# A planned transformer kernel: the opening's costs in the plan, the port shared by VectorE and GpSimd, and all orders chosen anew

## The chip, the cores and the metric

The kernel runs on one core of a Trainium2 chip. Each core has engines that work side by side, each through its own queue in order: TensorE (PE, with its weight loads PEld), VectorE (DVE), ScalarE (ACT), GpSimd (POOL) and SyncE (SP), which here issues the DMAs. The metric is the device time of one execution in microseconds (us); lower is better.

## The reference, cut to what matters

Two attention blocks over 2048 positions, 1024 channels and 32 heads of 32, whose outputs are concatenated.

```python
# A: four segments of 512; a causal softmax in the segment, and a memory of those before
q, k, v = x @ wq, x @ wk, x @ wv
for s in range(4):
    a_dot = softmax(qs @ ks.T * scale + mask) @ vs
    a_mem = (phi(qs) @ M) / (phi(qs) @ z + 1e-6)      # phi(t) = t + 1 if t > 0 else exp(t)
    o = g * a_mem + (1 - g) * a_dot                   # g = sigmoid(beta), one per head
    M, z = M + phi(ks).T @ vs, z + phi(ks).sum()
out_a = o @ wo
# B: linear attention with a learned feature map
q, k, v = split(x @ wqkv)
f = lambda t: concat(softmax(t @ w_phi), softmax(-t @ w_phi))   # per head
kv, z = f(k).T @ v, f(k).sum()
out_b = (f(q) @ kv) / (f(q) @ z + 1e-6) @ wo
```

## The kernel before, in words

Every large product is made of float16 halves: an operand is scaled by its largest magnitude, rounded to float16 (`hi`, on ACT), and what is left is rounded too (`lo`, on DVE or POOL); `product` then adds hi*hi, hi*lo and lo*hi in PSUM, so 128x128 by 128x512 is three matmuls. The B block's large products use a seven-product (Strassen) scheme, `strassen`, and A's output projection at the end another.

Stages in time: the opening (loads, scales and halves of the first segment and weights); the A block, 32 units of a segment and a group of four heads (`produce`, `attend`, with `fold`, which multiplies w_phi into B's weights, between them), up to about 850 us; B's pass over keys and values, up to about 1185; B's pass over queries, up to about 1515; A's output projection (L1719).

The order of the work is planned. Each operation is not issued where it is written but recorded by `op(engine, planned duration, function, r=reads, w=writes, prio=...)`. When all are recorded, `Graph.run` plays a greedy list schedule while the program is built: every engine is free from 0; again and again the operation that can start earliest is taken, among several the one of the smallest priority; its function then emits the instruction (or nothing, if it does nothing). So the plan fixes the order of each engine's queue and the PSUM banks, and on the chip the queues run in that order, each instruction waiting for its inputs. What the plan knows:

- durations, and latencies between engines (`LAT`: DVE to ACT 0.16 us, DVE to PE 0.4);
- for a DMA (engine SP): 0.6 us to issue, then its kilobytes over `FLOW` = 230 per us, one after the other, then `lat`;
- `port=True`: such a DVE operation and any POOL operation exclude each other, one starts after the other has ended;
- `NUDGE`: operations are counted off in stretches of 60; for a stretch with a number in `NUDGE` each priority is shifted by a pseudo-random amount drawn from that number, of a reach of 0.3 to 3.0;
- where PE would idle for over `GAP` = 0.5 us, `fill` inserts spare matmuls (L380) by a rule on how much PE has worked lately.

Instructions of the preparation (masks, the identity, the selector `sel`, cleared buffers: L337 to L377) are emitted before the graph and are unknown to its plan.

What the texts speak of in the opening: `load_seg(0)` loads the first segment of x in eight pieces (L469, `S<-ax`), reduces each to its largest magnitude (DVE L485) and then all (L495, `xam`); `scale` sums and spreads that with a matmul (PE L433) and makes the scale and its inverse (DVE L435, L437); `halves` makes hi (ACT L449) and lo (DVE L451). `load_wg(0)` does the same for the first group's key weights with ACT L491 (absolute sum), L433, L435, then POOL L443, ACT L445, POOL L446. `fold(-1)` loads `quad` (L1175) and scales it (L1192). The `stk` buffers get four constant rows each from `sel` (ACT L659, twelve copies). The first projection is `produce(0)`, L422. `phib` holds w_phi and is loaded by L1113 into a cleared buffer (L340); `mem` is A's memory (cleared at L1111).

Around 1190 us the sums of the keys, `za`, are turned into factors (`zr` L1508, L1510, L1511; `zs` L1513), the keys' product is scaled (L1516) and halved (ACT L1519, DVE L1521), and the queries' products (L618) and exponentials (DVE L1320 to L1330, ACT L1327, POOL L1624) begin; `keep` copies a product from PSUM (ACT L624). L1568 makes a scale of the output projection.

Of the kernel before, what the change touches and what calls it, by code (L numbers as in the profile page):

```python
# [12 lines left out]
AF = mybir.ActivationFunctionType  # L13
OP = mybir.AluOpType
AX = mybir.AxisListType
# [30 lines left out]
NUDGE = {0: 820989, 2: 102852, 3: 529656, 4: 266905, 5: 924189, 6: 435410, 9: 911235, 12: 450738, 13: 124130, 14: 669972,  # L46
# [59 lines left out]
class Graph:  # L106
# [36 lines left out]
    def op(self, eng, dur, fn, r=(), w=(), prio=0, lat=0.0, short=False, port=False, need=(), kb=256):  # L143
        o = Op()
# [163 lines left out]
def tile_kernel(ctx: ExitStack, tc: tile.TileContext, ax, aw, awv, awo, beta, bx, bwqk, bwv, bphi, bwo, out):  # L308
    nc = tc.nc
# [69 lines left out]
    G = Graph(pools)  # L379
# [14 lines left out]
    for i in range(NG):  # L394
        op(POOL, 0.358, lambda i=i: nc.gpsimd.tensor_tensor(
            bdm[:, i, :, 0:32], hd[:, :, None].to_broadcast([128, 4, 32]),
            gate[:, 4 * i:4 * i + 4, None].to_broadcast([128, 4, 32]), op=OP.mult), r=[gates], w=[(bdmb, i)], prio=0.3)
        op(DVE, 0.071, lambda i=i: nc.vector.tensor_reduce(bdm[:, i, :, 32], hd[:, :, None], axis=AX.X, op=OP.add), w=[(bdmb, i)], prio=0.3)
# [256 lines left out]

    stk = [G.buf("slot", [128, 2, 4, 512], F16, f"S{12 + i}") for i in range(3)]
    for t in stk:
        for h in range(4):
            op(ACT, 0.5, lambda t=t, h=h: nc.scalar.activation(t()[96:104, 1, h], sel[96:104, h:h + 1].to_broadcast([8, 512]), AF.Copy),  # L659
               w=[(t, (1, 3, h))], prio=0.3)  # L660
# [450 lines left out]
    op(POOL, 1.19, lambda: nc.gpsimd.memset(mem, 0.0), w=[phib, memb], prio=-1)  # L1111
# [24 lines left out]
    def fold(n, prio, dep=()):  # L1136
# [35 lines left out]
        if n < 0:  # L1172
# [18 lines left out]
            for k in range(4):  # L1191
                op(ACT, 0.5, lambda k=k: nc.scalar.activation(qd()[:, k], qd()[:, k], AF.Copy, scale=si()[:, 1:2]),  # L1192
                   r=[si], w=[(qd, k)], prio=0.5)
# [312 lines left out]
    for hb in range(2):  # L1506
        zr, zs, v = G.buf("b", [128, 8], F32, "zr", 2), G.buf("b", [128, 8, 2], F32, "zs", 2), slice(8 * hb, 8 * hb + 8)
        op(DVE, 0.172, lambda zr=zr, v=v: nc.vector.tensor_scalar(zr(), za()[:, v], 1e-12, None, op0=OP.max),  # L1508
           r=[(za, (hb, 0)), (za, (hb, 1))], w=[zr], prio=P)
        op(DVE, 0.12, lambda zr=zr: nc.vector.reciprocal(zr(), zr()), w=[zr], prio=P)  # L1510
        op(DVE, 0.141, lambda zr=zr: nc.vector.tensor_scalar(zr(), zr(), osc2[:, 1, 1:2], 2.0, op0=OP.mult, op1=OP.mult),  # L1511
           r=[(oscs, 1)], w=[zr], prio=P)
# [46 lines left out]
    def sizes_out(j, prio):  # L1559
        t = blocks(j, prio)  # L1560
        for k in range(2):
            for h in range(2):
                op(ACT, 0.614, lambda k=k, h=h: nc.scalar.activation(
                    t[k]()[:, h], t[k]()[:, h], AF.Abs, accum_out=ast()[:, 4 * j + 2 * k + h:4 * j + 2 * k + h + 1]),
                   w=[(t[k], h), (ast, (j, k, h))], prio=prio)
        if j == 3:
            scale((ast, ast), 16, (wscs, (2, 0), lambda: wsc[:, 2, 0]), prio, "s", 13)
            op(DVE, 0.1, lambda: nc.vector.tensor_tensor(wsc[:, 2, 1, 0:1], wsc[:, 2, 0, 0:1], osc2[:, 0, 0:1], op=OP.mult),  # L1568
               r=[(wscs, (2, 0)), (oscs, 0)], w=[(wscs, (2, 1))], prio=prio)
# [243 lines left out]
```

## Time and profile before

| | us |
|---|---|
| median of 3 runs (lowest, highest) | 1667.47 (1667.42, 1668.37) |
| the profiled execution | 1668.69 |
| its span | 1667.0 |
| PE busy | 1648.0 |
| DVE, ACT, POOL busy | 1357.1, 1111.7, 1059.3 |

The span reaches from the first instruction to the end of the last; the rest of the execution's time lies around it. In rows of instructions: start, length, engine, line, operation, out<-in, shape, count, and in brackets the engine's idle time before it with what ended it. Rows of one kind in sequence are merged into one (x8). A matmul's length holds its way through the array, so the distance between starts tells the rate.

### The profile page before, as it was taken

The numbers are of one execution on the slowest core, as the hardware profiler recorded it, in microseconds if no ns is written. First come the engines' busy times: TensorE is split into PE (matmuls) and PEld (weight loads), VectorE is DVE, ScalarE is ACT, GpSimd is POOL, SyncE is SP. The second block draws the span as 40 slices with busy tenths as digits, with TensorE's granted clock in tenths as the row PEclk, the third lists the DMA queues.
The fourth block names the chain that finished last, engine by engine and source line by source line (L and its number), as shares of the span: only waits on it lengthen the run. The fifth ranks groups of instructions, "written<-read, shape, count | busy, mean of one in ns | idle before, by whom it ended". The sixth has DMA issues, their size and how long they took to land.

```text
span 1667.0 us, 35571 instructions
## 1 busy us (share of the span) xinstructions
PE 1648.0 (99%) x12922; PEld 967.2 (58%) x12922; DVE 1357.1 (81%) x3213; ACT 1111.7 (67%) x2044; POOL 1059.3 (64%) x1393
## 2 busy tenths in 40 slices
PE   8999999999999999999999999999999999999999
PEld 7666767667676666766754444445544444444444
DVE  6899989899896888897877898988997787975441
ACT  8798779868787777777865767645755464454431
POOL 3967577576777886967874454545799897640000
PEclk9999999999999999999999999999999999999999
DMA  6845556779456462756566354276466665753311
GB/s 232 239 139 157 154 158 171 202 201 247 111 161 164 131 176 90 197 190 179 155 203 260 121 197 170 86 255 246 173 151 150 166 181 158 214 149 136 121 57 64
DMA packets 265599, 279.68 MB, mean 168 GB/s; under 512 B 162768, under 2 KB 216016, under 8 KB 256848
## 3 DMA queue, kind: packets, MB, share of 16 engines
q1 hardware_dynamic: 265424, 277.42, 56.0%
q8 instruction: 101, 1.65, 0.4%
q14 instruction: 74, 0.61, 0.1%
HBM read 143.34 MB, written 85.00 MB: 137 GB/s over the span
## 4 chain that ended last, share of the span: by engine, by line
PE 73%; DVE 10%; POOL 8%; ACT 4%; DMA 2%; issue 2%; SPq 0%; DVEq 0%; ACTq 0%; POOLq 0%
PE proj L422 25%; PE proj L618 11%; PE misc L422 6%; PE proj L1719 5%; PE s L1034 4%; PE pv L1070 4%; PE s L941 3%; PE s L618 3%; PE s L1719 2%; POOL e L1624 2%; PE misc L618 2%; POOL e L1636 1%; DVE mx L1320 1%; PE misc L1215 1%; PE misc L1719 1%
## 5 line engine op out<-in xcount | busy, mean ns | idle before, releaser
L422 PE MATMUL proj<-S,S 128*128 128x512 f16 (+1 forms) x2304 | 494.1, 343 | 0.6 <-ACT S L449 0.2
L422 PEld LDWEIGHTS <-S 128*128 128x128 f16 x3072 | 288.1, 98 | 160.3 <-ACT S L449 0.7
L618 PE MATMUL proj<-S,S 128*128 128x512 f16 x1488 | 344.2, 380 | 5.8 <-ACT cs L624 4.7
L618 PEld LDWEIGHTS <-S 128*128 128x128 f16 x1968 | 187.5, 98 | 220.1 <-issue 9.1
L1047 POOL TENSOR_SCALAR_AFFINE_SELECT ph<-ph 128x256 f16<-128x256 f16 (+1 forms) x448 | 194.7, 458 | 109.2 <-DVE ph L1041 94.9
L1041 DVE SCALAR_TENSOR_TENSOR ph<-s,ph 128x512 f16<-128x512 f32 x320 | 208.5, 683 | 51.7 <-ACT ph L1040 46.0
L947 DVE CUSTOM_DVE_ANT_0 s<-s,causal 128x384 f32<-128x384 f32 (+3 forms) x512 | 241.1, 509 | 8.5 <-PE s L941 5.9
L1040 ACT ACTIVATE ph<-s 128x512 f16<-128x512 f32 x320 | 185.3, 647 | 0.7
L422 PE MATMUL misc<-S,ot 128*128 128x512 f16 x768 | 171.0, 379 | 0.0
L1327 ACT ACTIVATE e<-e,sk 128x256 f32<-128x256 f32 x256 | 114.2, 497 | 61.1 <-DVE e L1324 39.9
L422 PEld LDWEIGHTS <-ot 128*128 128x128 f16 x768 | 73.8, 98 | 88.3
L1038 ACT ACTIVATE s<-s,bdl 128x512 f32<-128x512 f32 x160 | 105.7, 702 | 21.4 <-PE s L1034 21.1
L1038 ACT ACTIVATE s<-s,bd 128x512 f32<-128x512 f32 x160 | 103.0, 689 | 20.9 <-PE s L1034 14.9
L1034 PE MATMUL s<-S 104*128 104x512 f16 (+3 forms) x512 | 113.2, 299 | 0.0
L941 PE MATMUL s<-S 96*128 96x512 f16 (+3 forms) x512 | 112.0, 299 | 0.7 <-DVE dm L994 0.3
L422 PE MATMUL proj<-wv,S 128*128 128x256 f16 x768 | 101.2, 272 | 0.0
L1070 PEld LDWEIGHTS <-ph 128*128 128x128 f16 x2560 | 88.8, 96 | 18.8 <-POOL ph L1047 0.8
L1624 POOL TENSOR_TENSOR e<-e,zb 128x512 f32<-128x512 f32 x64 | 84.1, 1329 | 16.2 <-DVE r L1330 13.2
L1070 PE MATMUL pv<-vl,ph 128*128 128x66 f16 (+1 forms) x2560 | 92.2, 184 | 0.0
L1330 DVE TENSOR_REDUCE r<-e 128x32 f32<-128x1024 f32 x64 | 76.5, 1204 | 12.3 <-ACT e L1327 12.0
L618 PE MATMUL s<-S,S 128*128 128x512 f16 x324 | 78.6, 379 | 0.4 <-DVE S L451 0.4
L947 DVE DVE_READ_ACCUMULATOR2_ANT mt<- 128x1 f32 x512 | 71.7, 140 | 0.0
(375 smaller groups left out, 3303.2 us busy)
## 6 DMA issues: line engine op xcount, KB each, us to landing
S<-h SPq DMA_DIRECT2D x192, 128.0 KB
S<-wf_d SPq DMA_DIRECT2D x21, 1024.0 KB
st<-bwqk SPq DMA_DIRECT2D x56, 256.0 KB
wf_d<-fo SPq DMA_DIRECT2D x48, 256.0 KB
out<-os SPq DMA_DIRECT2D x38, 256.0 KB
wf_d<-oT SPq DMA_DIRECT2D x36, 256.0 KB
S<-xf_d SPq DMA_DIRECT2D x9, 1024.0 KB
S<-aw SPq DMA_DIRECT2D x16, 512.0 KB
```

The lines of the kernel that those rows point to most:

```text
L422: op(PE, dur, lambda c=c, a=a, b=b, lv=lv, rv=rv: nc.tensor.matmul(pv(), lv(), rv(), start=(c == 0 and a + b == 0), stop=(c == n - 1 and a ...
L618: op(PE, 0.2165, lambda n=n, a=a, b=b, lv=lv, rv=rv: nc.tensor.matmul(ps(), lv(), rv(), start=(start and n == 0 and a + b == 0), stop=(n = ...
L941: nc.tensor.matmul(ps()[:, o:o + 128 * i + 128], st()[0:96, 0, h, 128 * i:128 * i + 128], st()[0:96, 1, h, 0:128 * i + 128], start=True, s ...
L947: dve({128: 0.216, 256: 0.381, 384: 0.6, 512: 0.648}[n], lambda h=h, i=i, o=o, n=n: nc.vector.tensor_tensor_reduce(ps()[:, o:o + n], ps()[ ...
L1034: nc.tensor.matmul(ps()[:, o:o + n], st()[0:104, 1, h, 128 * j:128 * j + 128], st()[0:104, 0, h, 128 * j:512], start=True, stop=True)
L1038: act(0.571, lambda: nc.scalar.activation(ps(), ps(), AF.Exp, bias=0.0, scale=bd()[:, 4, i2, 0:1]), r=[(bd, i2)], w=[ps])
L1040: act(0.478, lambda: nc.scalar.activation(ph()[:, 0], ps(), AF.Copy, scale=2.0 ** 14), r=[ps], w=[(ph, 0)])
L1041: dve(0.6, lambda: nc.vector.scalar_tensor_tensor(ph()[:, 1], ps(), 2.0 ** 14, ph()[:, 0], op0=OP.mult, op1=OP.subtract), r=[ps, (ph, 0)], ...
L1047: nc.gpsimd.affine_select(pd, pd, pattern=[[0, n], [1, 128]], compare_op=OP.is_ge, fill=0.0, base=0, channel_multiplier=-1)
L1070: nc.tensor.matmul(ps()[:, i, n0:n1], ph()[:, a, o:o + 128], vl()[:, j, h4 + h, n0:n1], start=(i == 0 and a == 0), stop=(j == min(i, 2)), ...
L1624: op(POOL, 1.23, lambda a=a, h0=h0, e=e: nc.gpsimd.tensor_tensor(e()[:, 8 * a:8 * a + 8], e()[:, 8 * a:8 * a + 8], zv()[:, h0:h0 + 8], op= ...
L1719: op(PE, 0.2165, lambda n=n, a=a, b=b: nc.tensor.matmul(ps(), v(a)[:, n, :], wform[w]()[:, b, n, :], start=(start and n == 0 and a + b == ...
```

## The change

No instruction is added or taken away; the durations and dependences of the plan change, and with them the order of the queues (the number of filling matmuls may differ too).

- DMAs of a priority of -2 or below (the opening's): 0.47 us to issue, 0.65 of their kilobytes, 0.5 us more to land.
- Five stand-ins with no instruction, first in the plan: DVE 3.5 us, which "writes" `sel` and which the L659 copies now wait for; POOL 1.4 us, which "writes" `phib`, and 0.9; PE 0.8; ACT 0.5. The clearing of `mem` no longer stands as a writer of `phib`.
- L398 is planned at 0.1 instead of 0.071, L1192 at 0.62 instead of 0.5.
- L1508, L1511 and L1568 have `port=True`.
- All of `NUDGE` is another set of numbers (149 stretches before, 154 after).

```diff
-NUDGE = {0: 820989, 2: 102852, 3: 529656, 4: 266905, 5: 924189, 6: 435410, 9: 911235, 12: 450738, 13: 124130, 14: 669972,
...
+NUDGE = {0: 410426, 4: 742560, 5: 453547, 8: 418033, 11: 31061, 12: 825983, 13: 702578, 14: 361939, 15: 102890, 16: 584341,
...
     def op(self, eng, dur, fn, r=(), w=(), prio=0, lat=0.0, short=False, port=False, need=(), kb=256):
+        if eng == "SP" and prio <= -2:
+            dur, kb, lat = 0.47, 0.65 * kb, lat + 0.5
...
-        op(DVE, 0.071, lambda i=i: nc.vector.tensor_reduce(bdm[:, i, :, 32], hd[:, :, None], axis=AX.X, op=OP.add), w=[(bdmb, i)], prio=0.3)
+        op(DVE, 0.1, lambda i=i: nc.vector.tensor_reduce(
+            bdm[:, i, :, 32], hd[:, :, None], axis=AX.X, op=OP.add), w=[(bdmb, i)], prio=0.3)
...
+    selb = G.fixed(sel)
+    op(DVE, 3.5, lambda: None, w=[selb], prio=-99)
     stk = [G.buf("slot", [128, 2, 4, 512], F16, f"S{12 + i}") for i in range(3)]
     for t in stk:
         for h in range(4):
             op(ACT, 0.5, lambda t=t, h=h: nc.scalar.activation(t()[96:104, 1, h], sel[96:104, h:h + 1].to_broadcast([8, 512]), AF.Copy),
-               w=[(t, (1, 3, h))], prio=0.3)
+               r=[selb], w=[(t, (1, 3, h))], prio=0.3)
...
-    op(POOL, 1.19, lambda: nc.gpsimd.memset(mem, 0.0), w=[phib, memb], prio=-1)
+    op(POOL, 1.4, lambda: None, w=[phib], prio=-99)
+    op(POOL, 0.9, lambda: None, prio=-98)
+    op(POOL, 1.19, lambda: nc.gpsimd.memset(mem, 0.0), w=[memb], prio=-1)
+    op(PE, 0.8, lambda: None, prio=-99)
+    op(ACT, 0.5, lambda: None, prio=-99)
...
-                op(ACT, 0.5, lambda k=k: nc.scalar.activation(qd()[:, k], qd()[:, k], AF.Copy, scale=si()[:, 1:2]),
+                op(ACT, 0.62, lambda k=k: nc.scalar.activation(qd()[:, k], qd()[:, k], AF.Copy, scale=si()[:, 1:2]),
...
         op(DVE, 0.172, lambda zr=zr, v=v: nc.vector.tensor_scalar(zr(), za()[:, v], 1e-12, None, op0=OP.max),
-           r=[(za, (hb, 0)), (za, (hb, 1))], w=[zr], prio=P)
+           r=[(za, (hb, 0)), (za, (hb, 1))], w=[zr], prio=P, port=True)
...
         op(DVE, 0.141, lambda zr=zr: nc.vector.tensor_scalar(zr(), zr(), osc2[:, 1, 1:2], 2.0, op0=OP.mult, op1=OP.mult),
-           r=[(oscs, 1)], w=[zr], prio=P)
+           r=[(oscs, 1)], w=[zr], prio=P, port=True)
...
             op(DVE, 0.1, lambda: nc.vector.tensor_tensor(wsc[:, 2, 1, 0:1], wsc[:, 2, 0, 0:1], osc2[:, 0, 0:1], op=OP.mult),
-               r=[(wscs, (2, 0)), (oscs, 0)], w=[(wscs, (2, 1))], prio=prio)
+               r=[(wscs, (2, 0)), (oscs, 0)], w=[(wscs, (2, 1))], prio=prio, port=True)
```

31 rows, old and new, of the table NUDGE are left out of this document.

## The prediction

> **What bounds the kernel now.** I read the head and the chain of the profile first, then the busy time by stretches, then the two stretches in which TensorE is idle, engine by engine.
>
> ```profile
> span 1667.0 us, 35571 instructions
> PE 1648.0 (99%) x12922; PEld 967.2 (58%) x12922; DVE 1357.1 (81%) x3213; ACT 1111.7 (67%) x2044; POOL 1059.3 (64%) x1393
> PE 73%; DVE 10%; POOL 8%; ACT 4%; DMA 2%; issue 2%; SPq 0%; DVEq 0%; ACTq 0%; POOLq 0%
> ```
>
> TensorE (PE) is the bound: busy for 1648.0 of 1667.0 us. The change emits no instruction and removes none, so it can only move TensorE's idle time, its clock, and its warming and filling products. Where the idle time lies (columns: stretch, length, busy time of PE, of the weight loads, of DVE, ACT, POOL, the granted clock, DMA):
>
> ```profile
> 0.00:17.06 17.06, 13.11 (x78) 12.85 (x79) 9.01 (x24) 11.49 (x21) 8.72 (x17) 0.90 0.91 320
> 17.06:60.00 42.94, 42.07 (x285) 28.37 (x282) 33.77 (x126) 34.73 (x66) 25.18 (x36) 1.00 0.62 197
> 60.00:1180.00 1120.00, 1114.34 (x9641) 698.44 (x9640) 978.91 (x2564) 839.64 (x1565) 773.83 (x1064) 1.00 0.59 176
> 1180.00:1225.00 45.00, 40.70 (x305) 22.93 (x304) 43.79 (x78) 26.65 (x60) 32.11 (x37) 0.96 0.49 141
> 1225.00:1550.00 325.00, 324.86 (x2102) 153.64 (x2100) 249.85 (x366) 163.59 (x282) 219.47 (x242) 1.00 0.59 162
> ```
>
> The first projection starts at 17.06 us; what PE does before is warming, filling and a few small sums, so nearly all of these 17.06 us is lost. After that PE idles 0.87 us up to 60, 5.66 us in the 1120 us up to 1180, 4.30 us in the 45 us around 1200 (where the keys' pass hands over to the queries' pass), and 0.14 us up to 1550. The prize is thus two places and a thin rest of some 6 us.
>
> **The opening.** First what TensorE waits for, then ACT, DVE and the loads:
>
> ```profile
> 10.06 0.38 PE L433 MATMUL misc<-wgb,one 128*128 128x1 f32 x2 [1.79 <-ACT S L491]
> 15.58 0.28 PE L433 MATMUL misc<-xam,one 128*128 128x1 f32 x2
> 17.06 0.38 PE L422 MATMUL proj<-S,S 128*128 128x512 f16 x1
> ...
> 4.59 4.24 ACT L659 ACTIVATE S<-sel 8x512 f16<-8x512 f32 x8 [2.53 <-DVE sel L372]
> 8.86 1.06 ACT L491 ACTIVATE S<-S 128x1024 f16<-128x1024 f32 x1
> ...
> 4.95 0.69 DVE L485 TENSOR_REDUCE twb<-S 128x1 f32<-128x512 f32 x1 [0.40 <-DMA S<-ax]
> 6.64 0.69 DVE L485 TENSOR_REDUCE twb<-S 128x1 f32<-128x512 f32 x1 [1.00 <-DMA S<-ax]
> 10.47 0.16 DVE L435 TENSOR_SCALAR wgs<-misc 128x1 f32<-128x1 f32 x1 [3.15 <-PE misc L433]
> 10.75 3.63 DVE L485 TENSOR_REDUCE twb<-S 128x1 f32<-128x512 f32 x6
> 14.41 0.16 DVE L495 TENSOR_REDUCE xam<-twb 128x1 f32<-128x8 f32 x1
> ...
> 0.79 0.39 SPq L469 DMA_DIRECT2D S<-aw  x1
> 1.24 0.89 SPq L469 DMA_DIRECT2D S<-ax  x2
> 2.17 0.92 SPq L1113 DMA_DIRECT2D phib<-bphi  x2
> 3.14 3.82 SPq L469 DMA_DIRECT2D S<-ax  x6
> 11.00 0.33 SPq L1175 DMA_DIRECT2D quad<-bwqk  x1
> ...
> 1.70 4.92 DMA S<-ax
> 6.63 0.33 SPq L469
> ...
> 11.01 3.13 POOL L443 TENSOR_SCALAR S<-S,wgs 128x512 f32<-128x512 f32 x2 [6.96 <-DVE wgs L437]
> ```
>
> Read from the end. The projection at 17.06 needs x halved, which needs the largest |x| (L495, 14.41), which needs eight reductions (L485), one for each load of x. Two of them ran as their loads landed; then DVE stood 3.15 us at L435, the scale of the first weights, with six reductions queued behind it, which then ran back to back. L435 waited for the product at 10.06, that for ACT's absolute sum L491 at 8.86, and L491 stood behind eight copies of L659, which could not start before DVE had made `sel` (4.59, after 2.53 us of waiting). So eight copies that nobody needs yet, put ahead by a plan that believes DVE free at zero, hold up the scale chain for 4.24 us.
>
> What does the data allow? The chain of work has the third load land at 6.62 and the eleventh issue at 6.63: an issue waits for the landing eight issues before it. The issue at 11.00 is the nineteenth, so it waited for the eleventh, the last piece of x: that landed at about 10.98. A reduction takes 0.69, so the last one could end near 11.7 instead of 14.38 (10.75 + 3.63): 2.7 us. The weights were issued at 0.79, ahead of all x; if they landed no later than the third load, L491 could start by 6.62 instead of 8.86, L435 would follow near 8.2 (10.47 less 2.24), and the six reductions behind it would end at 12.1: still 2.2 us gained. If they landed with the first load of x, which released the reduction at 4.95, the landing at 10.98 alone sets the end.
>
> What the edits do there, each by itself:
> - The 3.5 us stand-in on DVE, which writes `sel`, with the copies reading it: in the plan the copies are ready at 3.66, not 0. L491 and the copies now come in an order that knows of it. This is the edit that can win the 2.7 us. The twelve copies keep their time; ACT has idle time for them until the halves begin at 16.29.
> - Loads of the opening at 0.47 us an issue instead of 0.6: the trace has two issues in 0.89 and two in 0.92. Bytes at 0.65: 256 KB become 0.72 us in the plan instead of 1.11; between the landings at 6.62 and 10.98 lie six loads of x and two small ones, 4.36 us or 0.73 a load of x. The plan's x now lands about when the chip's does, so reductions are queued where the data are. Worth nothing alone; the 2.7 us need it, since with the old rates the plan would expect x later than it comes.
> - The stand-ins on POOL (1.4 and 0.9), PE (0.8) and ACT (0.5) and the freeing of the `phib` loads from the clearing of `mem`: they shift planned starts only; POOL sat idle for 6.96 us before 11.01, which covers any of these shifts. Nothing, and without that cover at most the 1.19 us at which the plan priced the clearing.
> - 0.62 for the four scalings L1192 and 0.1 for the eight reductions L398: below, nothing.
>
> ```profile
> 37.44 2.55 ACT L1192 ACTIVATE quad<-quad,sif 128x512 f32<-128x512 f32 x4
> L398 DVE TENSOR_REDUCE bdm<-hd x8: 142/151/155, 37.4 to 52.9; 128x4 f32<-128x4 f32 x8
> ```
>
> They take 0.64 and 0.15 each; eight times 0.03 and four times 0.12 correct the plan by 0.7 us on engines that are not the bound there.
>
> Does a start 2.7 us earlier last? From 17.06 to 60 PE idles only 0.87 us, and its feeders in that stretch start from the same x scale, so they move with it. I take 2.7. Ends: 0 (a later load or POOL's weight chain holds PE at the old time) and 3.4 (also the 0.7 us that the product at 15.58 came after L495's end at 14.57 plus a semaphore).
>
> **The handover around 1190.** PE, the clock by stretches, then DVE beside POOL, then ACT:
>
> ```profile
> 1198.39 5.84 PE L618 MATMUL proj<-S,S 128*128 128x512 f16 x19 [2.26 <-ACT cs L624]
> ...
> 1194.79:1198.20 3.41, 1.33 (x7) 0.49 (x5) 2.87 (x7) 3.41 (x9) 0.00 (x0) 1.00 0.01 2
> 1198.20:1201.62 3.42, 3.23 (x8) 1.13 (x8) 3.42 (x6) 3.39 (x11) 3.29 (x4) 0.50 0.10 20
> 1217.40:1220.80 3.40, 2.05 (x14) 1.25 (x13) 3.40 (x9) 2.18 (x5) 0.72 (x2) 1.00 0.68 154
> ...
> 1188.46 1.09 DVE L1511 TENSOR_SCALAR zr<-zr,osc 128x8 f32<-128x8 f32 x1
> 1192.69 0.98 DVE L1508 TENSOR_SCALAR zr<-za 128x8 f32<-128x8 f32 x1
> 1188.25 2.50 POOL L1624 TENSOR_TENSOR e<-e,zb 128x512 f32<-128x512 f32 x2 [2.66 <-ACT zb L1500]
> 1192.05 1.59 POOL L1624 TENSOR_TENSOR e<-e,zb 128x512 f32<-128x512 f32 x1 [1.30 <-DVE r L1330]
> ...
> 1196.84 0.62 ACT L1519 ACTIVATE st<-ez 128x512 f16<-128x512 f32 x1
> 1197.76 0.58 ACT L624 ACTIVATE cs<-proj 128x512 f32<-128x512 f32 x1
> ```
>
> The plan prices L1511 at 0.141 and L1508 at 0.172. Beside POOL they took 1.09 and 0.98; the L1508 ended at 1193.67, just after POOL's product (1193.64). So DVE is 1.76 us later than planned, ACT's copies L1519 in their fixed order later too, and behind them stands L624, the copy that empties PE's bank: PE idles 2.26 us. Then the clock is granted at half: eight products in 3.42 us, where 48 elsewhere take 10.36:
>
> ```profile
> 994.08 10.36 PE proj L618 x48
> ```
>
> That is 1.7 us for the eight. The stall's bill is 2.26 + 1.7 = 4.0 us. With these operations marked as sharing POOL's port, the plan puts them after POOL's product, puts others ahead, and orders ACT by the true times. A stall of 1.35 us in the stretch from 1217.40 left the clock at 1.00, so I take the least change that spares the clock: 2.26 falls to 1.35 (0.9) and the half-rate stretch goes (1.7): 2.6. Ends: 0 and 4.0. The wait exists in the plan alone; but behind an operation that the plan places too late stand the reductions and subtractions of the queries' exponentials, and ACT's L1327 and L624 wait for those: DVE was busy for 43.79 of 45 us, so a misplaced one costs its 0.6 to 1.2 us again. L1568, marked too, frees nobody on PE's path: nothing.
>
> [...]
>
> **All orders chosen anew.** Every stretch gets another random shift, so the rest is drawn afresh. It can win at most the idle time that is there, 5.66 + 0.14 us, and can lose as much or more. Nothing in the trace tells the sign: I take 0, ends -2.9 (half of it) and +5.8 (the same again).
>
> **The sum.** The profiled execution took 1668.69: a span of 1667.0 and 1.69 around it. Less 2.7 and 2.6 it is 1663.4. The median of the runs, 1667.47, lies 1.2 below the profiled one: 1662.2.
>
> **Rivals.**
> - A. Both places win more: 3.4, 4.0, and the 1.35 us of the second stall, 8.8 less: 1658.7; with some of the thin rest, 1657. For it: the stall's cause is the mispriced step. Against: DVE is full there. 0.13.
> - B. The gain stays in the opening or gets lost: the x scale comes earlier, but PE then waits for the second weights, which POOL prepares (POOL busy 25.18 of 42.94), and the handover stalls in another way. 1665 (all but 0.2 of the opening's 2.7, nothing else) to 1667.5 (nothing). For it: lists are greedy, and one missing input stops a queue as before. Against: 0.87 us of idle time up to 60 shows no tight feeder. 0.26.
> - C. Slower: a new order lets PE stand over 2 us, with the half rate behind it, 4.0 us each by the handover's bill. One is less than the 5.3 forecast; from three on (12) the kernel is slower by over 0.2%: 1667.5 - 5.3 + 12.0 = 1674. In 1120 us the trace shows idle time of 5.66 in all and no half rate, which speaks against. 0.13.
>
> **Numbers.** A measurement tells about 0.2%, 3.3 us, from no change. Forecast 0.48 (own range 1659.5 to 1664), A 0.13, B 0.26, C 0.13. Faster: the forecast and A, 0.61; same: B; slower: C. The range from 1657 to 1668 leaves out C and a little of A and B, under 0.2 together.
>
> **What would show it.** Right: L491 ahead of most of the L659 copies and starting by 6.6; L495 near 12; the first projection near 14.4; no half rate near 1200. A half-rate stretch reaching past the first projection would cost up to 1.7 us. Wrong: the projection starts at 17 as before, or the first of PE's idle time moves to 17 to 60; PE idle in 60 to 1180 above 9 us would make C.

## The result, and the profile after

The changed kernel takes 1680.01 us (median; 1678.95 to 1680.97), the kernel before, on the same chip, 1667.92 (1667.42 to 1668.95): a ratio of 1.0072, 95% interval 1.0060 to 1.0085. It is slower by 12.1 us; the prediction said 1662.2. The profiled execution took 1680.19 with a span of 1678.5.

Head and chain of the profile after:

```profile
span 1678.5 us, 35518 instructions
...
PE 1648.9 (98%) x12902; PEld 961.8 (57%) x12902; DVE 1362.2 (81%) x3213; ACT 1114.3 (66%) x2044; POOL 1067.0 (64%) x1393
...
PE 35%; DVE 14%; POOL 6%; ACT 4%; issue 2%; DMA 2%; SPq 0%; ACTq 0%; DVEq 0%; POOLq 0%
```

TensorE is busy as long as before (1648.9 against 1648.0): no work was added, it only stands still more. By stretches, with the same columns and, but for the first projection's start, the same cuts as before:

```profile
0.00:16.08 16.08, 11.62 (x72) 11.24 (x73) 10.44 (x25) 12.93 (x23) 8.76 (x17) 0.92 0.90 318
16.08:60.00 43.92, 43.71 (x277) 27.93 (x278) 34.53 (x124) 34.55 (x67) 25.11 (x36) 0.95 0.66 203
60.00:1180.00 1120.00, 1104.67 (x9555) 689.90 (x9554) 966.73 (x2548) 834.80 (x1548) 763.37 (x1052) 1.00 0.57 174
1180.00:1225.00 45.00, 43.34 (x304) 24.28 (x302) 42.28 (x79) 29.48 (x68) 35.22 (x41) 1.00 0.51 170
1225.00:1550.00 325.00, 321.42 (x2125) 152.42 (x2124) 261.66 (x375) 162.76 (x283) 234.54 (x248) 1.00 0.58 163
```

Both places that the change aims at did improve: the projection starts at 16.08 instead of 17.06, and the handover has 1.66 us of idle time instead of 4.30, at full clock. But between 60 and 1180 TensorE idles 15.33 us instead of 5.66. Now set the instants of the two traces beside each other at equal work of TensorE done (the columns of its products, warming and filling ones left out; good to about half a microsecond). The changed kernel is 2.1 us ahead at 60, 2.5 behind at 300, 3.8 at 600, 9.0 at 900, 11.4 at 1180, 7.8 at 1200, 11.0 at the end. The loss comes in the long middle, bit by bit, which the change touched only through its new orders: the operations whose costs it corrected run before 60 or after 1180 us. Behind the handover it loses once more (3.58 us of idle time from 1225 to 1550 instead of 0.14); no experiment takes that stretch by itself.

The waits of TensorE from 60 to 1180 (line, what it waited for: us in total, times, longest); before, the two largest, and after, the six largest:

```profile
PE proj L618 <- ACT cs L624: 1.1, 1, 1.1
PE proj L618 <- ACT pq L624: 0.9, 2, 0.6
```

```profile
PE misc L975 <- DVE mh L970: 1.8, 1, 1.8
PE s L947 <- DVE mt L953: 1.5, 2, 0.8
PE proj L622 <- ACT pq L628: 1.5, 2, 1.0
PE s L1040 <- DVE ph L1047: 1.2, 2, 0.8
PE proj L622 <- ACT cs L628: 1.2, 2, 1.0
PE s L622 <- DVE S L455: 1.0, 1, 1.0
```

No single stall: many sorts of work, once or twice each, mostly ended by VectorE. Adding up the gaps over 0.1 us by what ended them gives VectorE 3.4 us before and 10.3 after, ScalarE 2.0 and 3.3, GpSimd none and 1.3.

### The profile page after: what moved, and what is told of

It is laid out like the page before. It is cut to its first block, busy times and chain, and to the rows that moved or that the text cites. A ratio compares the mean times of both kernels' runs of the same rounds, so it can differ in the third digit from the quotient of the medians.

```text
span 1678.5 us, 35518 instructions
## 1 busy us (share of the span) xinstructions
PE 1648.9 (98%) x12902; PEld 961.8 (57%) x12902; DVE 1362.2 (81%) x3213; ACT 1114.3 (66%) x2044; POOL 1067.0 (64%) x1393
## 4 chain that ended last, share of the span: by engine, by line
PE 35%; DVE 14%; POOL 6%; ACT 4%; issue 2%; DMA 2%; SPq 0%; ACTq 0%; DVEq 0%; POOLq 0%
PE proj L622 8%; PE proj L426 5%; PE misc L426 5%; PE proj L1729 5%; PE s L622 3%; PE s L1729 2%; DVE mx L1330 2%; DVE r L1340 2%; PE misc L622 1%; DVE e L1334 1%; PE misc L1729 1%; DVE e L1332 1%; POOL e L1634 1%; POOL e L1646 1%; DMA pt<-kls 1%
## 5 line engine op out<-in xcount | busy, mean ns | idle before, releaser
L426 PE MATMUL proj<-S,S 128*128 128x512 f16 (+1 forms) x2304 | 500.4, 344 | 0.5 <-DVE S L455 0.2
L1634 POOL TENSOR_TENSOR e<-e,zb 128x512 f32<-128x512 f32 x64 | 90.5, 1429 | 25.5 <-DVE r L1340 20.1
```

The lines of the kernel that those rows point to most:

```text
L426: op(PE, dur, lambda c=c, a=a, b=b, lv=lv, rv=rv: nc.tensor.matmul(pv(), lv(), rv(), start=(c == 0 and a + b == 0), stop=(c == n - 1 and a ...
```

## The experiments

**How the orders were taken apart.** The kernel before was built with its planner replaced by a list: the order in which a plan had issued the operations, their banks and fillers. With the list of either plan whole, the queues are those of the two kernels. A splice takes the operations that before's plan puts into a stretch in the order of the changed kernel's plan, and all others in before's; the seam is where the two orders meet. Line numbers there are before's plus 141.

```diff
     def run(self):
-        # greedy choice among the operations that can start
+        for k, i in enumerate(ORDER):          # a recorded order
+            ...                                # FILLS[k]: filler matmuls; BANKS: the recorded bank
+            self.ops[i].fn()
```

**1. Which stretch holds the loss.** ORDER is the changed kernel's for operations planned before 52 us (splice_O), from 52 to 1192 (splice_A), from 1192 to 1240 (splice_H), or in the first and third (splice_OH).

> The operations that the plan before starts in its first 52 us are queued in the order of the changed kernel, all others in the order of the kernel before. Theory (the loss lies in the orders chosen anew behind the opening): the trace pair has the changed kernel 2.1 us ahead at 60 us at equal work done, and nothing gives it back, so about 1665.8, 2 us faster than before. Rival 1 (an earlier start makes transfers and POOL collide later, and so loses whatever the order): 1668 or more, with the lead of 60 us gone by 200 us. Rival 2 (the opening wins nothing by itself): 1667.9.

> The order of the changed kernel only for what the plan before starts from 52 to 1192 us (A block and the pass over the keys); opening, handover and the rest in the order of the kernel before. Theory: this stretch carries the loss, from 2.1 ahead at 60 us to 11.4 behind at 1180 us in the trace pair, 13.6 us: about 1681. Rival 1 (the loss comes from the earlier start, not from this order): about 1668. In between, 1672 to 1676, if half of it belongs to the seams.

> The order of the changed kernel only for what the plan before starts from 1192 to 1240 us, the handover from keys to queries with the three operations that wait for POOL's port in the plan. Theory (this part of the prediction was right): the half-rate stretch near 1200 us goes and the kernel is 3 to 5 us faster, 1663 to 1665. Rival (the trace pair's 3.6 us there come from what PE was late with already, not from the order): 1667 to 1668, the stall of 2.3 us and the half rate stay.

> Opening and handover in the order of the changed kernel, the stretch between and all behind in the order of the kernel before: the two parts that were forecast, alone. Theory: both gains add up, 2.1 and 3 to 5 us, 1661 to 1663, as predicted for the whole change. Rival 1 (a gain in the opening is lost later whatever the order): 1663 to 1665, as the handover alone. Rival 2 (order of one stretch fits only its own neighbours): no gain, 1668 or more.

Measured, beside 1667.26 for before: splice_O 1669.14 (ratio 1.0008, interval 0.9999 to 1.0017), splice_A 1681.45 (1.0081, 1.0068 to 1.0094), splice_H 1668.76 (1.0006, 0.9997 to 1.0014), splice_OH 1666.73 (0.9996, 0.9987 to 1.0005). The middle stretch alone makes the whole loss and a little more, as its theory said. The two places that the change was drawn for move the time by nothing that can be measured: the theories of splice_O, splice_H and splice_OH (1665.8, 1663 to 1665, 1661 to 1663) all missed. At equal work splice_A is 3.3 us behind at 300, 2.6 at 600, 12.9 at 1180 and 13.4 at the end.

What became of the handover's gain, in splice_H (TensorE by stretches; the second row is the stretch that had the half rate before):

```profile
1180.00:1225.00 45.00, 44.48 (x331) 25.22 (x330) 43.60 (x80) 29.73 (x63) 35.84 (x38) 1.00 0.49 143
...
1198.20:1201.62 3.42, 2.99 (x15) 1.27 (x13) 3.42 (x7) 2.68 (x8) 1.95 (x4) 1.00 0.73 178
...
1224.00:1240.00 16.00, 14.52 (x69) 6.39 (x69) 15.43 (x27) 9.87 (x20) 14.77 (x17) 1.00 0.62 165
```

```profile
1230.56 2.75 PE L759 MATMUL proj<-S,S 128*128 128x512 f16 x12 [1.48 <-ACT cs L765]
```

```profile
1179.22 0.48 PE L1615 MATMUL kv<-ot,pt 128*128 128x65 f16 x10 [1.00 <-POOL pt L1608]
```

The stall of 2.26 us and the half rate are gone (clock 1.00), but the new order of this place pays for it on both sides. At 1179 TensorE waits 1.00 us for GpSimd; neither before nor splice_O has this wait, and all four splices with the new handover do. Behind the place it waits 1.48 us for the next copy out of PSUM, with VectorE busy 15.43 of 16 us. At equal work, against before's trace, splice_H is 0.9 us ahead at 1170, 0.9 behind at 1182, 2.8 ahead at 1200, 3.7 at 1225, 2.1 at 1240 and 0.7 at 1400: 4.6 won and all of it given back, 1.8 ahead of the place and 3.0 behind it.

**2. The opening and the clock.** In all traces of this case, but for their ends, the granted clock falls to half for 3.41 us (before, from 10.37 and from 1198.20) or for twice that (after from 13.66, splice_O from 13.46, splice_OF from 57.81). I call steps of 3.41 us, cut from the start of such a stretch, windows. Four of them in splice_O:

```profile
10.05:13.46 3.41, 1.91 (x15) 1.52 (x13) 2.17 (x6) 3.22 (x7) 3.41 (x3) 1.00 1.03 419
13.46:16.88 3.42, 2.41 (x10) 1.99 (x11) 1.82 (x3) 3.42 (x7) 1.23 (x2) 0.50 1.06 368
16.88:20.29 3.41, 3.41 (x9) 1.21 (x8) 3.41 (x6) 3.41 (x5) 0.00 (x0) 0.50 1.04 372
20.29:23.70 3.41, 3.41 (x26) 2.68 (x24) 3.00 (x14) 3.41 (x9) 0.59 (x3) 1.00 0.66 236
```

The first projections run at half rate: 9 matmuls in a window, 26 in the one after. splice_OF is splice_O with fillers in TensorE's two idle places before that, splice_OFH the same with the handover's new order; splice_OFH2 has half as many there and some at 57 us.

```diff
-FILLS = {553: (5, 4), ...}
+FILLS = {86: (10, 7), 94: (11, 7), 553: (5, 4), ...}                # OF, OFH
+FILLS = {86: (5, 7), 94: (5, 7), 520: (4, 7), 553: (5, 4), ...}         # OFH2
```

> The kernel before with the changed kernel's order in the opening alone (operations planned before 52 us), as in the earlier run of that splice, and now ten filler matmuls ahead of the product of x's largest values and eleven ahead of the second product of the weights' sums, where TensorE had stood idle for 1.2 and 1.3 us. Theory (the granted clock's half-rate stretch over the first projections, which follows those two gaps, ate the opening's gain): no half-rate stretch after 15 us, the first projections at 0.22 us each instead of 0.43, about 2.2 us less than the splice without fillers: 1666.9. Rival (the opening's gain is given back later whatever the clock does, at the waits near 56 to 60 us): 1669, no change to the splice without fillers.

> The changed kernel's order in the opening (with the same 21 filler matmuls) and in the handover (1192 to 1240 us), the order of before everywhere else. Theory (both places are worth what the traces of them showed, and they add): the earlier splice of both without fillers, 1666.7, less 2.2 us: 1664.5, under the kernel before by 2 to 3 us. Rival (nothing is left of a gain at the end of the program): 1666.7 to 1667.5.

> The order of before with the changed kernel's in the opening and in the handover, with half the filler matmuls of the run before (ten ahead of each of the two opening products, since each filler is two matmuls) and eight more ahead of the product that TensorE waits 0.9 us for at 57 us. Theory (the half-rate stretches follow TensorE's idle time in a window, so that with both places filled the clock stays up and the opening keeps its 2.2 us): 1664 to 1665.5. Rival (the earlier start is lost again at later waits, as in the run with twice the fillers): 1668 to 1674.

Measured, beside 1667.52: splice_OF 1674.42 (1.0038, 1.0024 to 1.0052), splice_OFH 1673.99 (1.0034, 1.0025 to 1.0044), its executions from 1669.82 to 1675.50; beside 1667.43: splice_OFH2 1668.03 (1.0005, 0.9997 to 1.0014). The theory held in the opening (no half rate there; 1.2 to 2.0 us ahead of the same order without fillers at 40 us) and failed for the time: splice_OF and splice_OFH came out above theory and rival both, splice_OFH2 at the rival's lower end. A filler call is two matmuls, so the first two kernels filled 2.1 and 2.3 us, more than the idle 1.2 and 1.3. And a half rate came later. splice_OF around 57 us:

```profile
54.40:57.81 3.41, 2.64 (x21) 2.15 (x20) 3.19 (x18) 3.41 (x8) 2.76 (x2) 1.00 0.88 305
57.81:61.22 3.41, 3.41 (x17) 3.07 (x16) 2.16 (x9) 3.06 (x5) 3.41 (x8) 0.50 0.98 235
61.22:64.64 3.42, 3.42 (x11) 1.47 (x10) 2.58 (x9) 0.95 (x2) 0.70 (x1) 0.50 0.71 139
```

Behind idle time of 0.77 us, which costs only itself in splice_O, stand 6.83 us of half rate here; at equal work the kernel goes from 1.5 us ahead at 50 to 2.2 behind at 80. splice_OFH, with the same idle time 0.7 us earlier in the program, kept its clock in the profiled execution (1.00 from 54.00 to 64.20). Its executions differ in this: the three with a mean clock of 1.000 took 1669.82 to 1671.60, the six with 0.998 took 1673.49 to 1675.50. With the idle time at 57 us filled too (splice_OFH2) the clock stayed at 1.00. Its fair partner is splice_H, which has the same handover and no half rate either. At equal work splice_OFH2 is 1.7 us ahead of it at 40, 1.1 at 400 and at 900, and level from 990 on, behind a wait of 0.97 us at 986 that splice_H does not have. So the earlier start was lost at a wait far behind it. No version that does the whole work came out under both kernels by more than the noise.

**3. Is the loss in one place, or only a shift?** Halves of the middle stretch, 52 to 600 (splice_A1) and 600 to 1192 us (splice_A2), and before's own order with its ten fillers ahead of the first projections made twenty (shift_b: `FILLS = {97: (10, 3), ...}` instead of `97: (5, 3)`).

> The order of before, with the changed kernel's order for operations planned between 52 and 600 us alone. The splice of the whole stretch 52 to 1192 us lost 13.4 us, 2.6 of them by 600. Theory (the loss is in the order of the operations, place by place): 1667.3 + 2.6 + about 0.5 at the new seam = 1670.4; the kernel's own plan, re-timed for this order, says +3.3. Rival (the loss is one of the second half alone, which only shows once other engines have fallen behind): 1667.3.

> The order of before, with the changed kernel's order for operations planned between 600 and 1192 us alone. The splice of the whole stretch 52 to 1192 us lost another 10.8 us between 600 and 1192. Theory (the loss is in the order, place by place, and the plan shows only part of it): 1667.3 + 10 to 11 = 1677 to 1678. Rival 1 (the chip follows the plan, re-timed for this order without the 65 ns that it books after each short matmul group, which the chip does not pay): +7.0, 1674.3. Rival 2 (the loss needs the first half's order ahead of it): within 2 us of 1667.3.

> The kernel before, order and all, with the planner's ten filler matmuls ahead of the first projections made twenty: TensorE starts its work 1.07 us later against the transfers, nothing else is changed. Theory (the time of one order hangs on the instants at which its operations fall, so that a shift of a microsecond changes waits and clock stretches hundreds of microseconds later): 1667.5 + 1.07 and another 1 to 5 us: 1669.5 to 1673.5, with new gaps far behind the opening. Rival (an order's time is its own, a shift is kept or absorbed at the next wait): 1667.5 to 1668.6.

Measured: splice_A1 1674.06 (1.0038, 1.0025 to 1.0050), splice_A2 1677.68 (1.0062, 1.0049 to 1.0074), shift_b 1669.10 beside 1667.86 (1.0010, 1.0001 to 1.0019). A1 came 3.7 us above its theory, A2 within it. They add to 16.7 us where the whole stretch cost 14.2; each half has a seam of its own, to which the plan, re-timed for these lists, gives up to about 4 us for the two. So the loss is spread over the stretch and not one event. shift_b lies between its theory and its rival; a start of TensorE a microsecond later does not bring the loss, its PE idle time between 60 and 1180 is 5.83 us, as good as before's.

**4. Is it this order, or any new one?** The changed kernel with other NUDGE tables: one searched on from its own (draw_aa), two searched from nothing (draw_a1c, draw_a2c), and one searched with a truer price (draw_p0), since the plan books 65 ns after each group of short matmuls, which the trace does not show (median 0.0 from L1070 to the next matmul).

```diff
-NUDGE = {0: 410426, 4: 742560, ...
+NUDGE = {...}                                                          # four other tables
...
-                free[e] += 0.065 if short and not o.short else 0.0
+                free[e] += 0.0 if short and not o.short else 0.0       # draw_p0 alone
```

> The changed kernel with another NUDGE table alone: 20 minutes' more search by the kernel's own planner from the table of the change, so that its plan ends at 1678.2 us instead of 1681.9 (before: 1680.9). Re-timed without the 65 ns that the plan books after each short matmul group and the chip does not pay, this order ends at 1669.6, before's at 1670.2, the changed kernel's at 1672.2. Theory (the chip runs an order within some us of its re-timed plan, and the order of the change was an unlucky one): 1665 to 1672. Rival (the order of before is the exception, and any newly chosen order costs about what its plan says): 1674 to 1680.

> The changed kernel with a NUDGE table searched from nothing, plan end 1685.3 (3.4 us over that of the change), re-timed without the 65 ns 1678.1 (5.9 over). Theory (chip within some us of the re-timed plan; before 2.9 under it, splices of the middle stretch 0.5 to 5.4 over it): 1675 to 1684. Rival (before the exception, plan decides): 1681 to 1687.

> As the draw before this one, another search from nothing: plan end 1682.7 (0.8 us over that of the change), re-timed without the 65 ns 1675.8 (3.6 over). Theory (re-timed plan): 1673 to 1681. Rival (plan decides): 1679 to 1685. How far the three draws lie from one straight line in either plan is what an order costs that no plan shows.

> The changed kernel with the planner's 65 ns after a short matmul group set to nothing and a NUDGE table searched for that price from the one of the change: plan end 1670.9, where before's order re-timed at that price ends at 1670.2 and the changed kernel's at 1672.2. Over the order so re-timed the chip took -2.9 us (before), +7.8 (after), +12.4, +13.4 and +12.8 (the three draws). Theory (a new order pays for chains of single operations that neither price shows): 1679 to 1684. Rival (the booked 65 ns hid the stalls, so that an order searched without it keeps its plan): 1668 to 1674.

Times in us (differences taken before rounding); "idle" is 1120 less the busy time of PE from 60 to 1180:

| order | plan's end | chip, median (ratio to before, interval) | chip less plan | idle |
|---|---|---|---|---|
| before | 1680.9 | 1667.5 | -13.4 | 5.66 |
| after | 1681.9 | 1680.0 (1.0072, 1.0060 to 1.0085) | -1.9 | 15.33 |
| draw_aa | 1678.2 | 1682.0 (1.0091, 1.0077 to 1.0105) | +3.8 | 17.89 |
| draw_a2c | 1682.7 | 1689.2 (1.0130, 1.0116 to 1.0144) | +6.4 | 17.14 |
| draw_a1c | 1685.3 | 1690.9 (1.0140, 1.0126 to 1.0154) | +5.7 | 17.40 |
| draw_p0 | 1670.9 at its own price | 1677.6 (1.0065, 1.0052 to 1.0079) | +6.6 | 14.97 |

Both theories missed upwards on the three draws; the direction is the rival's. The order of the change was no unlucky one: it is the best but one of five new ones, and what stands out is before's, the only one with idle time of 5.66 us. The five are not five independent draws: draw_aa and draw_p0 keep 127 and 116 of the 154 numbers of the change's table. Idle time is also not all that the draws lose: between 60 and 1180 the clock stood at half for 13.7 us in draw_aa, 6.8 in draw_a2c and 3.4 in draw_a1c, and for nothing in the other three. A plan 3.7 us shorter (draw_aa) ran 2.0 us longer. The booked 65 ns are not the cause either: searched without them, the plan ends where before's order re-timed does (1670.9 and 1670.2), and the chip takes 10 us more, 1.4 less than the theory's lower end.

**5. Is it VectorE's load, or ScalarE's?** Both in before's order (_b) and in splice_A's (_A):

```diff
-                    ps()[:, o:o + n], ps()[:, o:o + n], causal[:, 512 - n:512], 1.0, NEG, OP.add, OP.max,
+                    ps()[:, o:o + n // 2], ps()[:, o:o + n // 2], causal[:, 512 - n:512 - n // 2], 1.0, NEG, OP.add, OP.max,   # easeD
...
-nc.scalar.activation(ps(), ps(), AF.Exp, ...)
+nc.scalar.activation(ps()[:, 0:256], ps()[:, 0:256], AF.Exp, ...)                                                          # easeA
```

> The order of before in every queue; the 512 VectorE maxima of the scores go over half of their columns (so the other half of each block's keys is left out of the maxima), some 90 us less work on VectorE by the plan's prices. Both theories: this order has 3.4 us of TensorE's idle time ended by VectorE, so 1664 to 1667.5.

> The same half-width maxima under the order that puts the changed kernel's middle stretch (52 to 1192 us) into before, 1681.5 with full maxima, 13.4 over before. Theory (VectorE's queue runs late there by its load, 11.0 us of TensorE's idle time are ended by it): the distance to the same kernel in before's order falls from 13.4 to 6 us or less. Rival (chains of single operations, PE to VectorE to PE, set the gaps whatever the load; the re-timed plan keeps its 5.9 us with these prices): 11 to 14 us stay.

> The order of before; the 320 exponentials of the scores on ScalarE go over 256 of 512 columns (the others stay raw scores, and the scale of their two halves is 2^6 instead of 2^14), some 73 to 85 us less work on ScalarE. Both theories: 1664 to 1667.5.

> The same half-width exponentials under the order with the changed kernel's middle stretch. Theory (VectorE's load): the distance to the same kernel in before's order stays at 11 to 14 us, ScalarE ends only 3.0 us of TensorE's idle time there. Rival (VectorE's lateness is handed on from ScalarE, whose results half of its waits are for): it falls to 6 us or less.

Measured: easeD_b 1667.81 (1.0002, 0.9992 to 1.0011), easeD_A 1678.53 (1.0072, 1.0057 to 1.0087); easeA_b 1664.84 (0.9983, 0.9974 to 0.9993), easeA_A 1676.41 (1.0054, 1.0039 to 1.0069). The distance between the orders is 10.7 us with the lighter VectorE (just under the 11 to 14 of the rival, far from the 6 of the theory) and 11.6 with the lighter ScalarE (within the theory's 11 to 14), where it was 14.2 (splice_A). The stretch from 60 to 1180 in splice_A, easeD_A and easeA_A:

```profile
60.00:1180.00 1120.00, 1105.36 (x9555) 690.34 (x9554) 967.78 (x2548) 835.05 (x1548) 763.67 (x1053) 1.00 0.58 174
```

```profile
60.00:1180.00 1120.00, 1107.45 (x9576) 692.05 (x9576) 910.40 (x2553) 837.23 (x1554) 767.95 (x1056) 1.00 0.58 176
```

```profile
60.00:1180.00 1120.00, 1108.22 (x9594) 692.66 (x9593) 972.80 (x2557) 784.90 (x1558) 769.06 (x1059) 1.00 0.59 176
```

VectorE is 57 us less busy in the second, ScalarE 50 in the third, and TensorE's idle time of 14.64 falls only to 12.55 and 11.78. Neither of these two engines' loads carries the loss; some 3 us hang on either. GpSimd's load was not lightened in any run. What remains is when single operations run, which is argued from the traces below.

**What single operations do.** The largest gap after (1.79 us at 481.72) shows one way. VectorE, then GpSimd:

```profile
478.24 0.17 DVE L967 TENSOR_SCALAR_CACHE_REDUCE mh<-mt 128x16 f16<-128x16 f32 x1
478.46 3.21 DVE L970 SCALAR_TENSOR_TENSOR mh<-mh,mt 128x16 f16<-128x16 f16 x1
...
478.14 1.16 POOL L533 TENSOR_TENSOR fo<-quad,fo 128x512 f16<-128x512 f32 x1
479.25 1.16 POOL L901 TENSOR_TENSOR pkh<-pk,pkh 128x512 f16<-128x512 f32 x1
480.36 1.26 POOL L889 TENSOR_TENSOR pq<-pq,z 128x512 f32<-128x512 f32 x1
```

An operation on 16 columns, planned at 0.1 us with `port=True`, took 3.21 us: it ended at 481.67, when the third of three GpSimd products that run without a pause had ended (481.62). TensorE's next matmul needed it. The line's durations (least, median, largest, ns), after and then before:

```profile
L970 DVE SCALAR_TENSOR_TENSOR mh<-mh,mt x32: 114/178/3207, 56.8 to 867.8; 128x16 f16<-128x16 f16 x32
```

```profile
L964 DVE SCALAR_TENSOR_TENSOR mh<-mh,mt x32: 109/186/1219, 57.0 to 863.7; 128x16 f16<-128x16 f16 x32
```

In draw_aa the same operation took longer still (it ended at 482.26, the fourth of four GpSimd products beside it at 482.22), and stretched operations with `port=True` end most of TensorE's waiting for VectorE:

```profile
477.97 4.29 DVE L976 SCALAR_TENSOR_TENSOR mh<-mh,mt 128x16 f16<-128x16 f16 x1
```

```profile
PE kv L1490 <- DVE pt L1483: 4.8, 4, 2.0
PE misc L981 <- DVE mh L976: 3.7, 2, 3.3
```

The plan keeps the two apart, but by its own clock; the chip's times leave that clock (chip less plan is -13.4 to +6.6 us in the table), and the operation comes at another moment in GpSimd's queue. For every wait for VectorE I took the VectorE operations that ran without a pause up to it and counted what they took over their form's usual duration, where that is over 0.25 us, at most the wait. This gives about 1.8 of 3.4 us before, 5.3 of 10.3 after, 4.7 of 11.0 in splice_A, 10.1 of 15.5 in draw_aa, 7.6 of 11.4 in draw_p0. The total of stretched time is about the same before and after (34.8 and 34.2 us): what differs is whether TensorE waits behind it. This is read from the traces, not tested: no run kept GpSimd from working beside these operations. The other half of VectorE's waits are single gaps of 0.1 to 0.9 us behind operations of usual length (amem, oall, mt, ph near 842 to 858 us), for which the runs name no cause beyond the order.

## Why the prediction was wrong, point by point

- **The opening's chain: right, up to the projection.** The absolute sum (now L495) starts at 4.34, ahead of the copies, and the largest |x| (L499) is there at 11.91, near the forecast 12:

```profile
4.34 1.06 ACT L495 ACTIVATE S<-S 128x1024 f16<-128x1024 f32 x1 [2.28 <-DMA S<-aw]
...
11.91 0.16 DVE L499 TENSOR_REDUCE xam<-twb 128x1 f32<-128x8 f32 x1
...
13.17 1.04 ACT L495 ACTIVATE S<-S 128x1024 f16<-128x1024 f32 x1
...
14.21 4.38 ACT L453 ACTIVATE S<-S,xsc 128x512 f16<-128x512 f32 x7
14.35 0.59 PE L437 MATMUL misc<-wgb,one 128*128 128x1 f32 x2 [1.07 <-ACT S L495]
...
16.08 5.13 PE L426 MATMUL proj<-S,S 128*128 128x512 f16 x13
```

- **"Does a start 2.7 us earlier last? I take 2.7": wrong.** Of 2.7 only 0.98 reached the projection, and part of that is chance: before's profiled execution has a half rate over its warming products (first row below; the other rows are after's), and the same order without one starts its projection at 16.38 (splice_H) instead of 17.06. The rest was held up: ScalarE's queue has the second weights' absolute sum (13.17) ahead of x's halves (14.21), and TensorE's has the product that waits for that sum ahead of the projection. Then a half rate took it. The prediction named this ("a half-rate stretch reaching past the first projection would cost up to 1.7 us") and left it out of the sum; it stood from 13.66 to 20.49 and cost about 2.2 (half of the 4.41 us from the projection's start on). And the start of splice_OFH2, at 15.43 with the clock kept, did not last either.

```profile
10.37:13.78 3.41, 3.41 (x17) 3.41 (x17) 3.27 (x8) 2.46 (x5) 2.77 (x2) 0.50 1.08 369
...
10.25:13.66 3.41, 1.80 (x14) 1.41 (x13) 2.11 (x6) 3.34 (x7) 3.39 (x4) 1.00 1.01 417
13.66:17.08 3.42, 2.73 (x11) 2.14 (x12) 2.13 (x4) 3.42 (x7) 0.83 (x1) 0.50 1.08 376
17.08:20.49 3.41, 3.41 (x10) 1.21 (x8) 3.41 (x8) 3.41 (x5) 0.01 (x1) 0.50 1.03 373
```

- **The handover: mechanism right, size at the place right, its end wrong.** L1508 and L1511 (now L1518, L1521) take 0.16 and 0.22 us instead of 0.98 and 1.09, no half rate follows, and some 3.7 us are won from 1182 to 1200 where 2.6 were forecast. That the half rate goes is no accident: of eleven traces with before's order here, seven have a half-rate stretch between 1190 and 1215, of nine with a new one none. But it was never sure either: splice_O has the same stall (2.25 us) at full clock. The condition in the text, that in a full VectorE a misplaced operation costs again, is what came behind the place; the new wait for GpSimd ahead of it (1.00 us in splice_H, 0.80 after) the prediction did not have. Together they took all that was won, and splice_H shows no gain.

```profile
1198.95 0.16 DVE L1518 TENSOR_SCALAR zr<-za 128x8 f32<-128x8 f32 x1
...
1201.39 0.22 DVE L1521 TENSOR_SCALAR zr<-zr,osc 128x8 f32<-128x8 f32 x1
```

- **"All orders chosen anew ... I take 0, ends -2.9 and +5.8": the step that failed.** It measured +13.4 us at equal work (splice_A), more than twice the upper end. The error was to take the idle time that the old order has, 5.66 us, as the measure of what a new order would have. It is a property of that order: five others, with plans of the same length within some us or shorter, have 14.97 to 17.89. The value 0 assumed that before's order was an ordinary draw. Why that order runs 13.4 us under its plan stays open: how its table was found is not on record, and one that was kept because it ran well on the chip would be better than most; no run tests this.

- **Rival C had the sign and not the mechanism.** Its sign (PE idle above 9 us between 60 and 1180) is there with 15.33. But it priced stalls of over 2 us with a half rate behind each; after has no half rate between 60 and 1180, no gap over 1.8 us, and 31 gaps of over 0.1 us, 14.9 in all. Its mechanism does exist: in draw_aa a gap of 3.33 us ends at 482.32, within a half rate from 481.48 to 488.31.

- **The clock.** The prediction went by two windows of before: one busy for 1.33 of 3.41 us, with a half rate behind it, and one with a stall of 1.35 us that left the clock at 1.00. Half rates also follow one of 1.80 (after, 10.25 to 13.66) and one of 2.64 (splice_OF). Nor do they start at one instant: the opening's half rate starts at 13.66 after, 13.46 in splice_O and 14.38 in splice_OH, whose opening is in the same order; before's starts at 10.37, and splice_H's trace, whose opening is before's, has none (mean clock 1.000).

## What to carry to other kernels

When a change lets a planner choose all orders again, price the new draw by what such draws cost, not by the idle time of the order at hand: an order that runs well is rarer than a short plan: five whose plans lie within 5 us of before's (each at its own price; three of them kin) ran 10 to 23 us longer. Time a cost model's corrections with the order held fixed elsewhere, as the splices do, to see what they are worth by themselves, and keep the old order where it is good. Time won early is only kept if the queues behind it have no wait set by something else; follow it at equal work to the end, and beside a trace whose clock agrees: two profiled executions of the same opening differ here by 0.7 us at the first projection.

## What the runs showed of the hardware that was not expected

A VectorE operation of 16 columns, with a median of 0.18 us, took 3.21 us beside three GpSimd products in a row (after, L970) and 4.29 us beside four (draw_aa), and ended 0.05 and 0.04 us after the last of them. TensorE went to half rate behind a window busy for 2.64 of 3.41 us (splice_OF), though two windows of before, cut in steps of 3.41 from its half rate at 1198.20, kept it at full with 3.04 and 2.43:

```profile
1215.27:1218.68 3.41, 3.04 (x17) 1.73 (x16) 3.41 (x6) 0.07 (x1) 2.64 (x2) 1.00 0.84 176
1218.68:1222.09 3.41, 2.43 (x12) 1.07 (x11) 3.41 (x7) 2.12 (x5) 1.41 (x3) 1.00 0.37 82
```

From 55.06 to 57.40 splice_OF has, beside the idle 0.77 us, only products of 1, 2 or 128 columns, which the profile counts as busy; its busy time alone does not tell which windows a half rate follows, and the runs do not settle what does. splice_O's window at the same instants, twelve steps of 3.41 behind its half rate at 13.46, was just as busy, mostly with products of 512 columns, and kept the clock:

```profile
54.40:57.81 3.41, 2.64 (x17) 1.59 (x15) 3.19 (x13) 2.45 (x6) 1.73 (x2) 1.00 0.76 207
```

Half rate came in stretches of one window (3.4 us, before) or of two (6.8 us, after, splice_O and splice_OF), the second behind a first that was busy for 2.41 of 3.42 us (splice_O), 2.73 (after) or 3.41 of 3.41 (splice_OF); before's single ones were busy for 3.41 and 3.23.
